# Seventh feature chunk of a token-mixing product as half-width products on TensorE column tiles

## The chip, the cores and the metric

The kernel runs on one core of one Trainium2 chip. The metric is device time in microseconds (us) of one execution. Most executions of one kernel agree within 0.3%. Every comparison of times below is made on one chip, against runs of the kernel before in the same series; traces of different series come from different chips. "Span" is the profiled stretch from the first to the last instruction of one execution; the device time is longer than it by 1.7 us or more, and I call that remainder the time outside the span. It is known to about 0.05 us only, because the spans of unprofiled executions are listed to 0.1 us.

## The reference

The program is a linear-attention block followed by a gated MLP that mixes tokens. Only the last part matters for the change (S = 2048 tokens, D = 512, F/2 = 896 features):

```python
def _B_ref(x, w_in, w_sp, b_sp, w_out):
    z  = _gelu(jnp.einsum('bsd,df->bsf', x, w_in))
    z1 = z[..., :Fh].copy()
    z2 = _layernorm(z[..., Fh:], axis=-1)
    g  = jnp.einsum('ts,bsf->btf', w_sp, z2) + b_sp[None, :, None]   # token mixing
    return jnp.einsum('bsf,fd->bsd', z1 * g, w_out)
...
h  = x + _A_ref(_layernorm(x), A_wqkv, A_wo)        # attention
h2 = h + _B_ref(_layernorm(h), B_w_in, B_w_sp, B_b_sp, B_w_out)
```

The token mixing is a product of 2048x2048 by 2048x896.

## The kernel before

The 896 features are seven chunks of 128. Six of them go in pairs through `cell`, which computes the 2x2 block product (two feature chunks, two token groups of 512) with seven half products instead of eight; the operands `t1, t2, t4` and `s1, s2, s4` are sums of blocks. The seventh chunk has no partner, and is multiplied plainly: sixteen matmuls for each of its token groups.

```python
    cnt = [0, 0]

    def gate(fc, tok, b, add):                     # VectorE: g = product + bias; z1 * g
        t, z = u_t[cnt[0] % 2], z1T[:, fc, tok]
        ...
    for p in range(NG // 2):                       # two halves of the work
        lo, hi = (slice(tg * GW, (tg + 1) * GW) for tg in (p, p + NG // 2))
        last = KF - 1
        for tok, b in ((lo, EB[0]), (hi, EB[1])):  # the seventh chunk, plain
            matmuls(bank(b), [(z2[:, s, last * P:KF * P], wsp[:, s, tok]) for s in range(NT)])
            gate(last, tok, b, bsp[:, tok])
        ...                                        # t1, t2, t4
        for k in range(HF):
            ...                                    # s1, s2, s4
            cell(k, lo, hi)                        # seven products on two chunks
```

Every engine runs its instructions in the order of one packed list of operation numbers, which is written into the kernel and was searched for by a tuner:

```python
ORDER = "c-jTQ17HvU00h8C..."   # (cut) order in which the operations are put on the engines
```

And TensorE is kept busy at the very start by 50 warm-up matmuls whose result nobody uses.

```python
    def warmup(n, ns, behind=None):
        def fn(pe):
            for _ in range(n):
                inst = pe.matmul(bank(7, P), lhsT=warm, rhs=warm, start=True, stop=True)
            return inst
        ...
    warmup(34, 103)          # and 16 more behind the first statistics
```

## Time and profile before

| | kernel before |
|---|---|
| device time, median of 3 | 230.52 us (229.92 to 230.79) |
| span of the profiled execution | 228.4 us |
| TensorE / VectorE / ScalarE busy | 97% / 76% / 48% |
| share of TensorE in the chain that ended last | 87% |
| token mixing, first and second half | 112 to 163 us, 163 to 205 us and beyond |

TensorE bounds the kernel; the prediction below shows the lines that say so. The cost that it takes for VectorE comes from this row of the groups (line, engine, operation, output and inputs, shapes, count, then busy us and mean ns of one, then idle time before it and what ended it):

```profile
L996 DVE TENSOR_TENSOR u<-psum,bsp 128x512 bf16<-128x512 f32 x16 | 11.0, 688 | 9.4 <-PE psum L402 9.2
```

An addition of 128x512 out of PSUM takes 688 ns. The records of some matmuls are missing from this trace (1168 of 1191), so counts of matmuls are not compared.

### The profile page before, as it was taken

The page shows a single profiled execution, that of the slowest core. Times are in us where ns is not written, and L with a number is a line of the kernel's source. Part 1 is how long each engine was busy: PE and PEld are TensorE (multiplying, and loading weights), DVE is VectorE, ACT ScalarE, POOL GpSimd, SP SyncE. Part 2 cuts the span into 40 slices and gives each one's busy share as a digit, 9 for nine tenths or more (in the row PEclk, how much of TensorE's full clock was granted, in tenths as well). Part 3 has the DMA queues.
Part 4 walks back from the last instruction along what each step waited for, and adds up shares of the span by engine and source line. Part 5 has one row for each costly group of instructions (what it writes and reads, how often), then busy time and mean ns, then how long its engine had stood idle before and what let it go on. Part 6 is the DMA issues. An engine that isn't in the chain of part 4 may idle for free.

```text
span 228.4 us, 3248 instructions
## 1 busy us (share of the span) xinstructions
PE 221.9 (97%) x1168; PEld 110.1 (48%) x1191; DVE 174.5 (76%) x349; ACT 108.5 (48%) x203; POOL 47.1 (21%) x134
## 2 busy tenths in 40 slices
PE   7999999999999999999999999999999999999995
PEld 7444444453344444544444444444455556555453
DVE  3899656638999786679998869864988985574395
ACT  5695753389989988999762010300021311122010
POOL 4444300000562694138820000000000000000000
PEclk9999999999999999999999999999999999999999
DMA  6736449927566244599904999200000002010004
GB/s 192 240 77 139 93 110 377 252 70 182 115 126 129 46 95 92 115 210 187 182 1 90 196 192 203 58 0 0 3 0 0 24 26 92 0 46 3 0 23 161
DMA packets 58896, 23.68 MB, mean 104 GB/s; under 512 B 48512, under 2 KB 58752, under 8 KB 58880
## 3 DMA queue, kind: packets, MB, share of 16 engines
q1 hardware_dynamic: 58176, 22.88, 44.2%
q10 hardware_dynamic: 704, 0.59, 0.9%
q8 instruction: 9, 0.15, 0.3%
q14 instruction: 7, 0.06, 0.1%
HBM read 7.47 MB, written 2.10 MB: 42 GB/s over the span
## 4 chain that ended last, share of the span: by engine, by line
PE 87%; DMA 4%; DVE 3%; ACT 3%; issue 1%; POOL 1%; SPq 1%; DVEq 0%
PE psum L402 69%; PE psum L659 6%; PE psum L813 6%; PE psum L816 4%; DMA x<-in_A_x_dram 2%; DMA hnT<-hn 1%; DVE st L510 1%; ACT ct L421 1%; SPq L432 1%; ACT pqT L421 0%; PE psum L724 0%; PE psum L680 0%; ACT z L421 0%; DVE h L988 0%; ACT sh L421 0%
## 5 line engine op out<-in xcount | busy, mean ns | idle before, releaser
L421 ACT ACTIVATE psum<-psum 128x256 f32<-128x256 f32 (+1 forms) x39 | 17.7, 468 | 86.7 <-PE psum L402 55.5
L402 PE MATMUL psum<-wsp,z 128*128 128x512 bf16 x201 | 47.8, 379 | 0.4
L402 PEld LDWEIGHTS psum<-wsp,z 128*128 128x128 bf16 x208 | 20.3, 98 | 23.0
L421 ACT ACTIVATE e<-psum 128x1024 bf16<-128x1024 f32 (+1 forms) x18 | 16.7, 927 | 14.1 <-PE psum L402 13.1
L402 PE MATMUL psum<-t,s 128*128 128x512 bf16 x95 | 22.3, 379 | 0.1
L402 PE MATMUL psum<-wsp 128*128 128x256 bf16 (+1 forms) x87 | 18.9, 313 | 0.2
L421 ACT ACTIVATE z1T<-psum 128x512 bf16<-128x512 f32 x28 | 15.7, 600 | 6.3 <-PE psum L402 5.7
L996 DVE TENSOR_TENSOR u<-psum,bsp 128x512 bf16<-128x512 f32 x16 | 11.0, 688 | 9.4 <-PE psum L402 9.2
L813 PE MATMUL psum<-win,hnT 128*128 128x512 bf16 x63 | 16.4, 379 | 0.3 <-DMA hnT<-hn 0.3
L402 PE MATMUL psum<-wout,z1T 128*128 128x256 bf16 (+1 forms) x81 | 16.2, 313 | 0.0
L659 PE MATMUL psum<-pk,xn 128*128 128x512 bf16 x64 | 15.3, 379 | 0.0
L402 PE MATMUL psum<-xnT,wqkv 128*128 128x512 bf16 x61 | 15.1, 379 | 0.2
L402 PE MATMUL psum<-m,pqT 128*128 128x512 bf16 x62 | 14.6, 380 | 0.4 <-DVE h L787 0.2
L402 PE MATMUL psum<-wqkv,xnT 128*128 128x512 bf16 x61 | 14.7, 379 | 0.2
L421 ACT ACTIVATE z<-psum 128x896 bf16<-128x896 f32 x16 | 14.4, 919 | 0.8 <-PE psum L816 0.5
L402 PEld LDWEIGHTS psum<-t,s 128*128 128x128 bf16 x96 | 9.4, 98 | 10.0
L581 DVE TENSOR_SCALAR e<-e 128x1024 bf16<-128x1024 bf16 (+1 forms) x18 | 7.0, 391 | 8.1 <-ACT e L421 7.9
L816 PE MATMUL psum<-win,hnT 128*128 128x384 bf16 x64 | 13.0, 326 | 0.0
L510 DVE BATCH_NORM_STATS2 st<-x 128x6 f32<-128x512 bf16 x15 | 9.9, 674 | 3.8 <-DMA x<-in_A_x_dram 3.8
L996 DVE TENSOR_TENSOR u<-psum,p 128x512 bf16<-128x512 f32 x12 | 8.3, 688 | 5.8 <-PE psum L402 5.8
L787 DVE SCALAR_TENSOR_TENSOR h<-psum,x 128x512 bf16<-128x512 f32 x16 | 10.7, 686 | 1.8 <-PE psum L402 1.7
L402 PEld LDWEIGHTS psum<-wsp 128*128 128x128 bf16 x90 | 8.7, 98 | 6.8 <-DVE wsp L1001 0.4
(126 smaller groups left out, 378.3 us busy)
## 6 DMA issues: line engine op xcount, KB each, us to landing
r<-rcp SPq DMA_DIRECT2D x16, 128.0 KB, 2.6
out_dram<-h SPq DMA_DIRECT2D x15, 128.0 KB, 1.7
win<-in_B_w_in_dram SPq DMA_DIRECT2D x2, 896.0 KB, 7.2
x<-in_A_x_dram SPq DMA_DIRECT2D x6, 256.0 KB, 4.3
wqkv<-in_A_wqkv_dram SPq DMA_DIRECT2D x2, 512.0 KB, 5.7
wout<-in_B_w_out_dram SPq DMA_DIRECT2D x1, 896.0 KB, 7.2
wo<-in_A_wo_dram SPq DMA_DIRECT2D x1, 512.0 KB, 5.9
bsp<-in_B_b_sp_dram SPq DMA_DIRECT2D x1, 512.0 KB, 4.4
```

The costliest lines, as they stand in the source:

```text
L402: inst = pe.matmul(out_ap, lhsT=a, rhs=b, start=start and i == 0, stop=stop and i == len(pairs) - 1, **kw)
L421: return g.add("ACT", lambda ac: ac.activation(out_ap, in_ap, func, **kw), [in_ap, *extra], [out_ap] + ([accum] if accum is not None else []),
L432: return g.add(eng, lambda q: q.dma_start(out_ap, in_ap), [in_ap], [out_ap], cost=issue, lat=lat, dma=name, **k)
L510: dve(lambda v: v.bn_stats(s[:, 0:6], src[:, n, :]), [src[:, n, :]], [s[:, 0:6]], D)
L581: dve(lambda v: v.tensor_scalar(e, e, 1.0, EPS_PHI, op0=ALU.min, op1=ALU.add), [e], [e], w * GW, acc=4)
L659: inst = pe.matmul(bank(CB[c]), lhsT=xn[:, i, c * P:(c + 1) * P], rhs=pk[:, i, :], start=i == 0, stop=i == NT - 1)
L787: dve(lambda v, n=n, b=b, s=s: v.scalar_tensor_tensor(h[:, n, :], bank(b), 1.0, x[:, n, :], op0=ALU.mult, op1=ALU.add, accum_out=s[:, 0:1] ...
L813: pe.matmul(bank(b), lhsT=hnT[:, c, n * P:(n + 1) * P], rhs=win2[:, c, 0:GW], start=c == 0, stop=c == KD - 1)
L816: inst = pe.matmul(bank(b + 1, F2), lhsT=hnT[:, c, n * P:(n + 1) * P], rhs=win2[:, c, GW:FH], start=c == 0, stop=c == KD - 1)
L996: dve(lambda v: v.tensor_tensor(t, bank(b), add, ALU.add), [bank(b), add], [t], GW, ps=True)
```

## The change

The seventh chunk is split into two pieces of 64 features, so that it too becomes a 2x2 block product with seven half products instead of eight. A product with 64 output features uses only half of the array's columns, so two of them are to run side by side, one on the lower and one on the upper column tile. The partial sums that land in the wrong half of the partitions are moved by ScalarE copies. The intent is 28 matmul slots for 32 in each half of the work.

```diff
+    s6 = [g.sbuf(f"s{j}c", ...) ...]            # s1, s2, s4 of 64 features
+    b2 = g.sbuf("b2", ...)
@@
-    load_x("SP", 0, 1, 2150)
+    load_x("SP", 0, 1, 2200)                    # (and other assumed load times)
@@
+    def halves(pairs, extra):
+        def fn(pe):
+            for s in range(max(len(a) for _, a, _ in pairs)):
+                for o, a, start in pairs:       # the two tiles take turns
+                    if s < len(a):
+                        inst = pe.matmul(o, lhsT=a[s][0], rhs=a[s][1], ...)
+            return inst
+        ...
+    def last_cell(lo, hi):
+        halves([(pb(Y, L), [(z2[:, s, fl], wsp[:, s, lo]) for s in ss], True),
+                (pb(X, U), [(s2[:, s, :], t2[:, s, :]) for s in ss], True)], 106)
+        halves([(pb(E, L), [(s1[:, s, :], t1[:, s, :]) for s in ss], True),
+                (pb(Y, U), [(z2[:, HT + s, fh], t4[:, s, :]) for s in ss], True)], 106)
+        act(b2[U], pb(Y, L), ACT.Copy, GW)      # across the partition halves
+        dve(... pb(X, U) = pb(X, U) + b2[U] ...)
+        act(pb(X, L), pb(X, U), ACT.Copy, GW)
+        for r in (L, U):
+            add(p5[c][r], E, L, hi)
+        halves([... four and four ...], 106)
+        halves([... eight and eight ...], 106)
+        add(b2[L], E, U, lo)
+        add(b2[U], X, U, lo)
+        gate(KF - 1, lo, Y, b2)
+        gate(KF - 1, hi, X, p5[c])
@@
-        last = KF - 1
-        for tok, b in ((lo, EB[0]), (hi, EB[1])):
-            matmuls(bank(b), [(z2[:, s, last * P:KF * P], wsp[:, s, tok]) for s in range(NT)])
-            gate(last, tok, b, bsp[:, tok])
@@
         for k in range(HF):
+            if k == C6[p]:                      # behind the other cells
+                ...
+                last_cell(lo, hi)
@@
-ORDER = "c-jTQ17HvU00h8C..."
+ORDER = "c-jrsLjoiQ00h9s..."                    # a new order of everything
```

More of the change, by code (lines that the diff above doesn't have):

```diff
@@ L15 @@
 SEM_NS = 45.0
-ORDER = "c-jTQ17HvU00h8Cwq47%ZQHhO+qGrewr$(CZ5wxy5Czc?4-pX=Q4t+65EHQw8*z{Txe$On$c?;6f}{Y5a0rjk2m>Q5gkT7T2ndM~2##b(juc3VL`aNO$cOwWi~>lD3aEsNXo|{cjQB{1)JTIOD2Q~(fTBo`Ldb-SD2C$5iYlmz%xHpU$bxFfhMLHZ66k@F=!tIVj#8+O9H@a>sDtKcftF~6Ug(X!=!4d%jkYL_x~PXSD1)-7k8x;#u~>%jIE;f>jw3jPHfV>q$cb_&kM`(*0T_sW=#P%*gw9xkrI>(;n1rL4jAJ-~6<CSYScT)5f`({>!5D;*2*fl@#dHk8X#`;?hG7lXVH8HA3%X(kW@0`TU=~hdA<kee*5eeO<0W2TvYuj!o?$lTU^qr#12$q27Go23U_0hw9yVhO_F@lqVjp&4H_qZ5wqhI3V?Pey3a;WBF5n`r;|4C_CNAR^UgHg3;Vo|CF7DwD?&AT1^Bo={1Vi!>BJe#v;WIwq2fpDa9^(l@F)YI{G`}M}BQg>{;tRgw7yck7!GDOw*bK+t_={9b&8UpVD2&WJ%*_0Z!RXAw0!%|QE6I3_!?=vkv`okJ%)pGy%hD9fupslXEVD5?b1)|hu`r9UD2uTc%dswlu{?7zfC-q8nK)Isxr8lQn{8N}^;nY0)rxJ|gFTsuiCKY3n3N^BhP_#b^|_c!xr}Ssnx&YG$yt$=SeaGWfK}O$jo6q?Sc558jVaWesnnDy)rTp$g{ifNTiK3j)Qf$&m%}-NHQ9pI*`6KPk^R`8oj8D<*^E;d$n=`ZAdciVPUCcD)fvuUHxA?=4rUi-P)6<JC}z`Wj^RvZR$66II%QW*<<MEq;yRAya*pF{&f#2c=MK)}3XbPW9$_wJQf}o@KAqzP?&nZW;sGAydd_E8cIPxr<a7<=LQduoF5*!xU^30nOwH14&Cy)V(|j$^LM_rA=2Za|QehQQeic&*U13ob)G-#<U6xd7RaPl&U|GH4RbFFxz2$kn<9puYP9En8p5!i`;zk}~6CGwbRnQZbQ598GB|YUIR@WE)<uiWeH-=YmMNkM`;6FB14PE4OzThS9=4C?n`G60(iI4c5t5{VvRZCPIZDun?)CWe=YQE$vUgr(o<SqVSWJOU_N!CyP;zveTJyla}wNOjdReiNmYqe8I#ZY{;S99HF2X$5g1t_K-GnQg2m`*dHUh_9UF_c29joPY#x~QXis++p2lX|F;daJK?s-b$Rs~W4H`fGsVD6SGIng;1J2Wp7=D2&1?v63j9;_1AGX}B(EutsR4hH94rHA+dfQI|AYV>DLdwN;z6M-wzoleA8!wM}PqMf<c`o3&jJwL|N*Mr*ZS8+1{-bx>z@PJ4A!hqOfp^hk&GTu*dNM|4@obye4NLMQc9*Y!+6nyA})p&NRv@4BPAdaYA>qno;=#ag1JTBhY%p_N*tmx5pEp5E%6KI*<6=)FGahd$`1zUZ@R_?N!woBryz{wSqsIhgHK{-^p5?hx+i1`g>^4(%`w=SHsW2#)B~uIW0C=I9RV@UG>^j^Y@O=~%AnIF9XVuIK7*;<%3I_)g%2PU5Cc>}F2mhHmZvCvsY+b7v=WCntAfr*{TtbX{k5CTDSLXLnZTbT+qfZg+Jaw{;8Wa4r{gA?J5K7j{t>aTm9Aceipe7k4+8aA}uyNtbd@w{sbnb9;Ai4_9zy_jP&qbAR`8Z};(JPjMwr_h8TP5YO~%&+-5d^dL|3aZmMJ&+#zN^Fpupd~fgqZ}bR{^d@iiR&ViQFY*#^^G@&fcJFYIhkBRyc$CL_xJNtC<2>GDe8LmF)O)?p%e>zcJ;^71$_IVgXMENNyuvU1(yx5c%YEMGe8Go&#IJqSE4|jMyvC3H#Fu>8Pkq(bebcvn#n*hpw|vLXe9w3Nzz_Y_@BH2$oYW~?z<C|XQC-Cqeb~qR#_Rmt_r2PW{L%jbNviim"
@@ new lines @@
+ORDER = "c-jrsLjoiQ00h9stZm!2ZQHhO+qP}nwr$(CmAs)26&?{08L<%#5fBMc5Eao79Wf9Su@D#WkOR4p6S)Bpp%DUt5kN?UL2v{?A|ya!Bt#MfMKB~qG9*U|<UwBKLqViQ9K=UTq(XkALjj~gArwId6h>O4M`jd7IaEMKR780+Mng0~BUD0VG(|JCKyze56=XqmWJNJ_Ll+cBS9C`SR7EyaLk-kIYt%$bltgW`K`Ye3IFv$Zj7MFJ!C2J85-h_~EJt>fL0PmzTl7Fr^g?gcM+5XhUkpG$^v6I<KznpRM;yc<9L5n0#|VVNL`=pcOu;lv#R{y%Y8=He9LFl0Kv+!2It;>K48cf@!f13tXUxD%%*O%@#W0-28l1)~EW~Wg!FsI4DV)JGyu@Tp(Nj#-G`+w^Y``Wg!eVU44$Q?oY{nMs#UAX$F6_oxoWnkx$5w2^ejLCRT*Wn9z(ribO<cw;yv1w0!7JRxb=<&x+`}E*#RCLkPzK{WJj5fsM^c65Cw#zXJjN6J#7BI=H~c_2enohK{}7G8@CW2`gk&fNX9z}T41Px#{zhp2MPx=~Bt~EgiYb|qxtN!k7?n|&o2eL^aTt@an3`#rmg$(D`DkWl9_D8jW@R>JX9kvJfMr;UIarqQ7?(8|pS78jOW2$Vn2_aInl)LAi&=mLS%`&MgvD8hMcIO_Se_MFk(F4POId}j*^P;rgo&7x)!3cMn4CSihIQGJ%h-nXSf35pkd4@bYgvq2xRt%wo7>oy?bx0j*pbQAl#Mx*BRGsBIh><7nq#<}V>yo7xq~~og1fkq$&^A}Sb|kqoqIT)DV0il*^Es%gK0H|8I@X@G?kf^M$?!@S=EW@lwBE=US~L6Gn7L)l}9r*OS3gco!OPSG?UqMmgjh$eK?+d*^jf>pR+lElQ@T~IG6Kyf%7?l7nx7Fb%X_!SA|qi#Z*N3Rai$^RCichC3Tmjbc_SJkn6aQgSnmyIFUm*h;ucW6;(o|b%ka0hV!(D^OZykv`~vwN#%5vZ+VU7^@J7llx6jYfBB46^@U&gjmLR{8+ecR`GD8Ck(c<K`&mr~c#tP~h^zUI|9F}2`JJbDgCF>jHwiTo^@Fz<Mqw31)m1~4)mW!lOX1W+;nh@|_>hnIm@oK}uNXlQ6;xGJM>Q2i&D27*)m&{9M=e!XQ58%-`HR67LLnttq10B96iv4oSMAhM@wA)ql|Y9XT`{zot<+le)Jg5tU0u{w9n?(?)Kk6HSv}NH^|e{Q8Bk>PQ9>osC&pAP^;JKG)@u&XXU0}yt=4U=*A@*@FZI_+4bd<S)KHDkC~eblozh^9)=rJlSdG_F9n%_Z&_+$vIGxc1oz^66)eeo+Zk^M9-O*X?(pqiTCau!}9n>D})p6a`KAqPI-PZ#>(L-I-QytPJ9o9P?(MP@4WnIuC-P094(^Xy54ZYA!-O?vL)^oko8(r5cz1C-a)en8wFTK@Ieb5*E)?zKuQZ3VRt<XxX(m#Du5C`=iHL(0wcEBMV+`$~iO&r$Y+|)fB!Qma!p$+$PC^vLOM{+Yqb~MLu6i0P8$9617cTC51JST8MCvpoXF`d}Woy<u+)7_oiDV)-&oW{M~%30jl>D<~`o!;4<+G(B9nViEpoy)nM$BmrLJ)O^a-O~Bp#)VwO1zga@UCeD=*hO8&W!=FgUCQlT&gEUn?OnkYUD+Mo$$i|})m+0>+{Im8+kM^7{awogT-DWG)Ad}}13k!tJ;X!3(yKkpt9;bQeB38}!oxk=cfH2<Ji@1Z+9Q3&=Y7`GJ<8`i*5iD^<2~9FJ;pOU!IM1Ivpmgfz0Mas$CEw9>%GAneaV}>$#Xr=4}9PAy~Y3j&vU!CdV#lju@`!omw2fcdAV2kvUhricl)Yu__`nZkso`P_n3hz-s@}L=jVRnr@rOe-fsmC`;edcr(gJ`U-`9v`L_@FkKg#6Klqd1`n^B;yTAF1KRb@=xV}p}v*SC1OZevh;75GWe|^V490&vn1PufWe0A`^e|U=oX8"
@@ L315, in bass_sequential_preLN__linear_attn_block__mixer_gmlp__prompt_kernel @@
     HT, HF = NT // 2, KF // 2
+    O_ST = 1024
     TB, SB = HT * GW * 2, HT * P * 2
@@ L337, in bass_sequential_preLN__linear_attn_block__mixer_gmlp__prompt_kernel @@
             for k, o in enumerate((o_win + KD * FH * 2, o_win, o_pk + TB))]
+    s6 = [g.sbuf(f"s{j}c", o, [HT, P // 2], BF16) for j, o in enumerate((o_win + KD * FH * 2 + 3 * SB, o_win + 3 * SB, o_c + O_ST))]
+    b2 = g.sbuf("b2", o_pk + TB + 3 * SB, [GW], FP32)
+    assert TB + 3 * SB + GW * 4 <= KD * S * 2 and 3 * SB + HT * P <= KD * FH * 2
     p5 = [g.sbuf(f"p5{b}", o_ct + 2 * TB + b * GW * 4, [GW], FP32) for b in range(2)]
@@ L373, in bass_sequential_preLN__linear_attn_block__mixer_gmlp__prompt_kernel @@
     warm = const("warm", [P], BF16)
+    cc[0] = o_c + O_ST
     st = [const(f"st{k}", [NT, 8], FP32) for k in range(2)]
@@ L487, in load_x @@
         return first_load(eng, x[:, n:n + w, :], x_d[n * P:(n + w) * P, :], f"x{n}", lat, behind)
-    load_x("SP", 0, 1, 2150)
-    load_x("ACT", 1, 1, 2300)
-    x2 = load_x("SP", 2, 1, 2300)
-    load_x("ACT", 3, 1, 2550)
-    first_load("SP", wqkv[:, 0:2, D:2 * D], A_wqkv[0:2 * P, D:2 * D], "wka", 4200)
-    wk = first_load("ACT", wqkv[:, 2:4, D:2 * D], A_wqkv[2 * P:4 * P, D:2 * D], "wkb", 4400)
-    for n, lat, behind in ((4, 4600, None), (6, 3400, x2), (8, 3850, wk), (10, 4000, wk), (12, 4200, wk), (14, 4400, wk)):
+    load_x("SP", 0, 1, 2200)
+    load_x("ACT", 1, 1, 2350)
+    x2 = load_x("SP", 2, 1, 2350)
+    load_x("ACT", 3, 1, 2600)
+    first_load("SP", wqkv[:, 0:2, D:2 * D], A_wqkv[0:2 * P, D:2 * D], "wka", 4800)
+    wk = first_load("ACT", wqkv[:, 2:4, D:2 * D], A_wqkv[2 * P:4 * P, D:2 * D], "wkb", 5000)
+    for n, lat, behind in ((4, 5200, None), (6, 4000, x2), (8, 2500, wk), (10, 2700, wk), (12, 3700, wk), (14, 3900, wk)):
         load_x("SP", n, 2, lat, behind)
@@ L989, in mo_pair @@
             store(n, slice(0, D), h[:, n, :])
-    cnt = [0, 0]
+    cnt, C6 = [0, 0], (2, 2)
     def gate(fc, tok, b, add):
@@ L1023, in cell @@
         gate(k + HF, lo, B, bsp[:, lo])
+    def halves(pairs, extra):
+        def fn(pe):
+            inst = None
+            for s in range(max(len(a) for _, a, _ in pairs)):
+                for o, a, start in pairs:
+                    if s < len(a):
+                        inst = pe.matmul(o, lhsT=a[s][0], rhs=a[s][1], start=start and s == 0, stop=s == len(a) - 1,
+                                         skip_group_check=True)
+            return inst
+        return PE(fn, [v for _, a, _ in pairs for ab in a for v in ab], [o for o, _, _ in pairs], len(pairs[0][1]) * 216 + extra)
@@ new lines, in last_cell, with add @@
+    def last_cell(lo, hi):
+        c = cnt[1] % 2
+        cnt[1] += 1
+        X, Y, E = 6, 7, EB[c]
+        H = P // 2
+        s1, s2, s4 = s6
+        f0 = (KF - 1) * P
+        fl, fh = slice(f0, f0 + H), slice(f0 + H, f0 + P)
+        L, U = slice(0, H), slice(H, P)
+        ss = range(HT)
+        pb = lambda b, r: psum[r, b, :]
+        q = range(HT // 2)
+        def add(o, b, r, i):
+            dve(lambda v: v.tensor_tensor(o, pb(b, r), bsp[r, i], ALU.add), [pb(b, r), bsp[r, i]], [o], GW, ps=True)
+        halves([(pb(Y, L), [(z2[:, s, fl], wsp[:, s, lo]) for s in ss], True),
[3 more added lines that the diff above has]
+        act(b2[U], pb(Y, L), ACT.Copy, GW)
+        dve(lambda v: v.tensor_tensor(pb(X, U), pb(X, U), b2[U], ALU.add), [pb(X, U), b2[U]], [pb(X, U)], GW, ps=True)
+        act(pb(X, L), pb(X, U), ACT.Copy, GW)
+        for r in (L, U):
+            add(p5[c][r], E, L, hi)
+        halves([(pb(Y, L), [(z2[:, HT + s, fl], wsp[:, HT + s, lo]) for s in q], False),
+                (pb(E, U), [(z2[:, HT + HT // 2 + s, fl], wsp[:, HT + HT // 2 + s, lo]) for s in q], True)], 106)
+        halves([(pb(X, L), [(s4[:, s, :], wsp[:, HT + s, hi]) for s in ss], False),
+                (pb(X, U), [(z2[:, s, fh], wsp[:, s, hi]) for s in ss], False)], 106)
+        add(b2[L], E, U, lo)
+        add(b2[U], X, U, lo)
+        gate(KF - 1, lo, Y, b2)
+        gate(KF - 1, hi, X, p5[c])
@@ L1038, in bass_sequential_preLN__linear_attn_block__mixer_gmlp__prompt_kernel @@
         for k in range(HF):
+            if k == C6[p]:
+                if p == 0:
+                    f0, H = (KF - 1) * P, P // 2
+                    x11, x21, x12, x22 = (z2[:, s:s + HT, f0 + j * H:f0 + (j + 1) * H] for s in (0, HT) for j in (0, 1))
+                    combine(s6[0], x21, x22, ALU.add)
+                    combine(s6[1], s6[0], x11, ALU.subtract)
+                    combine(s6[2], x12, s6[1], ALU.subtract)
+                    combine(x21, x11, x21, ALU.subtract)
+                last_cell(lo, hi)
             if p == 0:
```

## The prediction

> **What bounds the kernel now.** I read the page first: the busy shares and the chain of work that ended last.
>
> ```profile
> span 228.4 us, 3248 instructions
> PE 221.9 (97%) x1168; PEld 110.1 (48%) x1191; DVE 174.5 (76%) x349; ACT 108.5 (48%) x203; POOL 47.1 (21%) x134
> ...
> PE 87%; DMA 4%; DVE 3%; ACT 3%; issue 1%; POOL 1%; SPq 1%; DVEq 0%
> ...
> L402 PE MATMUL psum<-wsp,z 128*128 128x512 bf16 x201 | 47.8, 379 | 0.4
> L402 PE MATMUL psum<-t,s 128*128 128x512 bf16 x95 | 22.3, 379 | 0.1
> ```
>
> The chain is 87% TensorE. The two groups at the end are most of the token mixing (products of `wsp` with the gated half `z`, and the combined operands `t`, `s` of six feature chunks), and TensorE idled 0.4 and 0.1 us before them. The mean of 379 ns is the length of one pipelined record; what a matmul costs is the distance between starts. In the timeline sixteen stand between 123.78 and 127.23 us, so 3.45 / 16 = 0.216 us each.
>
> ```profile
> 123.78 3.62 PE L402 MATMUL psum<-wsp,z 128*128 128x512 bf16 x16
> 127.23 3.62 PE L402 MATMUL psum<-t,s 128*128 128x512 bf16 x15
> 130.69 3.62 PE L402 MATMUL psum<-wsp,z 128*128 128x512 bf16 x16
> 134.14 3.62 PE L402 MATMUL psum<-t,s 128*128 128x512 bf16 x16
> ```
>
> The first and third rows are the seventh chunk of the first half of the work (its two token groups of 512, sixteen matmuls each); TensorE goes from row to row without a hole. A table by stage shows how near the other engines are:
>
> ```profile
> core 0: us, PE busy (x) PEld busy (x) DVE busy (x) ACT busy (x) POOL busy (x), PEclk, DMA share, GB/s
> ...
> 112.00:163.00 51.00, 50.74 (x235) 23.08 (x239) 40.93 (x66) 10.23 (x20) 3.49 (x8) 1.00 0.48 90
> 163.00:205.00 42.00, 41.79 (x236) 23.32 (x239) 33.44 (x61) 7.61 (x19) 0.00 (x0) 1.00 0.08 26
> ```
>
> Token mixing of the first half lies in 112 to 163 us, the second half after it, mixed with output products. TensorE is full at clock 1.00, VectorE 80% busy (40.93 of 51, 33.44 of 42), ScalarE nearly free. So a TensorE slot saved here is time saved, as long as VectorE keeps up.
>
> The kernel already has matmuls on column tiles, the best evidence for this change: sixteen products of 32 columns, four to a tile row, between ordinary ones (timeline of TensorE):
>
> ```profile
> 43.52 1.03 PE L659 MATMUL psum<-pk,xn 128*128 128x512 bf16 x4
> 44.48 1.05 PE L680 MATMUL psum<-pk,ones 128*32 128x512 bf16 x16
> 45.46 1.04 PE L659 MATMUL psum<-pk,xn 128*128 128x512 bf16 x4
> ```
>
> From 44.48 to 45.46 us sixteen matmuls took 0.98 us: four slots of 0.216 (0.863) and 0.12 left over. So four tiles share one slot. The ordinary four before take 43.52 to 44.48, 0.96 instead of 0.863: 0.10 left over. Going into tile mode and back thus costs 0.10 + 0.12 = about 0.21 us per visit.
>
> **What the Trainium skill says.** (1) "TensorEngine Tiling (Array Packing)", Key Properties: tiles work independently, and changing the tiling mode drains the engine. The trace agrees on both, at 0.21 us for in and out. (2) "TensorE: Matmul & The Clock Gate", Measured speedup vs the span model: three column tiles gave 2.38 times, not 3. The trace is kinder in a stream (four tiles in one 0.216 slot), and it decides. (3) "PSUM — Partial Sum Buffer", PSUM bank collisions raise a hardware error: column tiles may write disjoint partitions of one bank at the same time. The change relies on this; the trace has it for four tiles of one bank. (4) "VectorE: DVE Perf Modes", Why PSUM operands drop a tier: fp32 from PSUM runs at the basic rate. The trace has 690 ns for 128x512 out of PSUM. Lanes are parallel, so I take the same 690 for an operation on 64 partitions (estimate; no half-partition row exists).
>
> **The change part by part.**
>
> *TensorE, removed.* Two token groups of 16 matmuls in each of two halves: 64 slots, 64 x 0.216 = 13.82 us.
>
> *TensorE, added.* The chunk is cut in two pieces of 64 features, and the same seven-product scheme as in the other cells runs on it. A 64-column product of eight contraction blocks takes half the array; two run side by side. Per half of the work four calls: 8, 8, 4 and 8 pairs (seven products, the seventh split into two sums of four). That is 28 slots for 32. If pairs share a slot, both halves take 56 x 0.216 = 12.10 us: 8 slots or 1.73 us saved.
>
> *TensorE, mode visits.* Two groups per half could mean four visits. I decoded the instruction order in the diff and numbered it against the old list. On TensorE the first two calls are adjacent in the first half, while the third and fourth are separated by ordinary cells; in the second half the first two are separated and the last two adjacent. That is three visits per half, six in all: 6 x 0.21 = 1.26 us. Net on TensorE: 1.73 - 1.26 = 0.47 us saved.
>
> *VectorE.* Per half five new operations of 512 fp32 from PSUM (one partial sum added, two halves of p5, two halves of the other bias sum): 5 x 0.69 = 3.45 us. The gates keep their number. In the first half four new combinations of 8x64 bf16; the trace has 420 ns for 512 bf16 elements, so 1.7 us. VectorE becomes about 40.9 + 5.2 = 46.1 of 51 us (90%), and 33.4 + 3.5 = 36.9 of 42 (88%).
>
> *ScalarE.* Two copies per half across partition halves, 584 ns each: 2.3 us on an engine 20% busy there.
>
> *The chain inside a new cell.* After the second call: copy 0.58, add 0.69, copy 0.58, and in the second half two p5 additions ahead on VectorE, 1.38: about 3.2 us. TensorE has ordinary work and the third call in that time (about 3.4 us in the second half, over 9 in the first, counted in slots from the decoded order). This just closes in the second half.
>
> *Lost filler.* The 32 plain matmuls needed no combined operand, so they bridged the four 2.28 us combinations of `t` (2.28 us per record). Now the first cells must come without them; I estimate 0.2 us of holes.
>
> *Reordering elsewhere.* The diff also alters assumed load latencies, and the whole order with them: another order of first statistics, the third weight load ahead of the first transposes, and input weights after more `wsp` loads. Before 16 us TensorE is busy 14.00 of 16, much of it warm-up, so a better order might win a few tenths; the later queue could cost as much. I put -0.2 there, with +-0.5.
>
> Sum: -1.73 + 1.26 + 0.2 - 0.2 = about -0.5 us. From 230.5: 230.0.
>
> **The rivals.**
>
> *Tiles do not overlap.* Then 112 half-width matmuls cost 112 x 0.216 = 24.2 us for 13.8 before, plus 1.26: +11.6 us, 242 us. Speaking for it: no 64-column row in the trace, and twice as many weight loads per slot. Against: the 32-column rows, with four loads and four matmuls in each slot. I give it 1%.
>
> *VectorE or the copy chain becomes the bound.* At 90% in the first half, with products that wait for operands only VectorE makes, TensorE could stand still 1 to 3 us: 231 to 233 us. For it: the lost filler and 5.2 us of added work in 51. Against: TensorE never waited 0.2 us for VectorE in this stage before, and the chunk has moved behind cells that keep TensorE fed. I give it 15% for over 1 us.
>
> *The saving is swallowed by mode visits.* If a 64-column visit costs 0.29 us rather than 0.21, the gain is nil: 230.4 us. This is quite possible and would not be told from the prediction by the time alone.
>
> *The reordered loads decide.* With a net effect of half a microsecond, a moved weight or transpose can outweigh the title of the change in either direction: 229 to 231.5.
>
> **Range and chances.** All likely outcomes lie within 1.5 us of the old time; runs before span 229.92 to 230.79. A gain of 2% would need 4.6 us, but the whole saving without any cost is 1.73. A loss of 2% needs the first rival, or a bad second or fourth. I take 230.0, range 228.9 to 231.4, and chances 0.01, 0.96, 0.03.
>
> **What would show it.** In the changed profile: matmul rows 128*64 whose pairs start together, with 0.216 us from pair to pair (step one); six visits with some 0.1 us lost on each side (step two); no TensorE idle before `t,s` rows above a few tenths (filler); VectorE near 46 us in the first token mixing stage; the start of that stage moved by under 0.5 us against before (reordering). The prediction is wrong if pairs come 0.43 us apart, if TensorE waits on the partition-crossing copies or on `t`, or if the start of the stage moves by more than a microsecond.

## More of the kernel before

All runs used here are in the fast state. The one run without a state is a single look, and says so.

## The result, and the profile after

The changed kernel took 230.56 us (median of 6 runs, 230.11 to 231.18), the kernel before in the same series 230.37 us (6 runs, 229.55 to 230.79). The ratio is 1.0017, with a 95% interval from 0.9993 to 1.0042: the same within 2%, and hardly to be told from no change at all. Ratios here are the mean time of one kernel's fast runs over that of the other's of the same rounds, so not quite the ratio of the medians that I quote.

The page of the changed kernel, with the busy line and the chain that ended last:

```profile
span 228.4 us, 3395 instructions
PE 223.0 (98%) x1239; PEld 109.5 (48%) x1239; DVE 183.9 (81%) x363; ACT 110.5 (48%) x207; POOL 48.8 (21%) x134
...
PE 89%; ACT 4%; DVE 2%; DMA 1%; POOL 1%; issue 1%
```

The span is the same to a tenth, TensorE is as full as before, and VectorE went from 76% to 81%. In the groups, the new products are those of L1036, 64 columns wide:

```profile
L407 PE MATMUL psum<-wsp,z 128*128 128x512 bf16 x144 | 34.0, 379 | 0.0
L407 PE MATMUL psum<-t,s 128*128 128x512 bf16 x96 | 22.0, 379 | 0.0
...
L1036 PE MATMUL psum<-wsp,z 128*64 128x512 bf16 x48 | 9.6, 382 | 0.0
...
L1055 DVE TENSOR_TENSOR b<-psum,bsp 64x512 f32<-64x512 f32 x4 | 2.8, 694 | 4.4 <-PE psum L1036 4.4
...
L426 ACT ACTIVATE b<-psum 64x512 f32<-64x512 f32 x2 | 1.2, 589 | 9.7 <-PE psum L1036 9.7
```

No TensorE idle stands before any of these matmul groups, the plain ones or the new ones. This column hides small losses, though: it counts from the modelled end of the matmul before (a record is 379 ns long, while starts are 216 ns apart), so a loss of under 0.16 us shows only in the distance of starts. A VectorE addition on 64 partitions takes as long as one on 128 (694 against 688 ns), as the prediction had assumed. How two tiles share a slot is seen in the timeline of TensorE (start, length, instruction):

```profile
133.63 1.03 PE L407 MATMUL psum<-wsp,z 128*128 128x512 bf16 x4
134.58 0.40 PE L1036 MATMUL psum<-wsp,z 128*64 128x512 bf16 x1
134.59 0.40 PE L1036 MATMUL psum<-t,s1c 128*64 128x512 bf16 x1
134.82 0.38 PE L1036 MATMUL psum<-wsp,z 128*64 128x512 bf16 x1
134.83 0.38 PE L1036 MATMUL psum<-t,s1c 128*64 128x512 bf16 x1
```

And at the end of the same visit:

```profile
137.85 0.38 PE L1036 MATMUL psum<-t,s0c 128*64 128x512 bf16 x1
137.85 0.38 PE L1036 MATMUL psum<-t,z 128*64 128x512 bf16 x1
138.16 1.04 PE L407 MATMUL psum<-t,z 128*128 128x512 bf16 x4
```

The two matmuls of a pair start 0.01 us apart, and later pairs follow each other every 0.216 us. At the entry, though, the first pair starts 0.309 us after the last ordinary matmul instead of 0.216 (0.09 lost), and at the exit the next ordinary matmul starts 0.312 us after the last one on the tiles (0.10 lost). The first pair's slot is 0.240 us long and the first ordinary one afterwards 0.226 (0.03 lost). Where the ordinary neighbours have 256 columns, they lose as much. Added up from the starts, a visit costs 0.226 us, and the six cost 1.36 us. The expectations further down have 0.24 a visit and 1.43 for six, a first count of mine that was a little too high. The stages (same stretches and columns as in the prediction):

```profile
112.00:163.00 51.00, 51.00 (x265) 22.75 (x265) 47.07 (x74) 11.91 (x23) 3.52 (x7) 1.00 0.42 84
163.00:205.00 42.00, 42.00 (x260) 23.01 (x259) 34.33 (x67) 8.91 (x22) 0.00 (x0) 1.00 0.08 26
```

VectorE (third busy number) went from 40.93 to 47.07 us in the first stretch, and TensorE stayed full. So the result is a saving that was spent again on TensorE itself. To see where, I measured the distance between landmarks that both traces have (from the starts of single matmul records, in us):

| from / to | before | changed | difference |
|---|---|---|---|
| start to first key-sum product (`pk,ones`) | 44.48 | 44.47 | -0.01 |
| to first `win,hnT` matmul (first input product of the MLP) | 19.68 | 19.91 | +0.23 |
| to last `win,hnT` matmul | 43.05 | 43.04 | -0.01 |
| to last matmul: token mixing and output, "the stage" below | 118.29 | 118.13 | -0.16 |
| to the end of the span | 2.86 | 2.83 | -0.03 |

The column tiles act only in the fourth line. There the ledger closes: 8 slots saved are -1.73, six visits are +1.36, one new hole is +0.14 (0.13 and a first slot that is 0.01 longer), and small stalls at 146, 162 and 212 us are +0.06. The sum is -0.17; the trace has -0.16. The hole is this one (timeline of VectorE, then of TensorE's weight loads; the bracket gives the idle time before and its releaser):

```profile
106.44 0.51 DVE L560 TENSOR_SCALAR z<-z,st,rs 128x896 bf16<-128x896 bf16 x1 [0.72 <-POOL rs L523]
...
106.99 0.67 DVE L867 TENSOR_TENSOR psum<-psum,p5z 128x512 f32<-128x512 f32 x1
...
107.71 0.11 PEld L407 LDWEIGHTS psum<-wsp 128*128 128x128 bf16 x2 [0.35 <-DVE psum L867]
```

In the new order VectorE stands still for 0.72 us for a GpSimd result, and the sum behind it reaches TensorE too late. The kernel before has no such hole.

### The profile page after: what moved, and what is told of

The parts are those of the page before. It is cut to its first block, busy times and chain, and to the rows that moved or that the text cites. A ratio compares the mean times of both kernels' runs of the same rounds, so it can differ in the third digit from the quotient of the medians.

```text
span 228.4 us, 3395 instructions
## 1 busy us (share of the span) xinstructions
PE 223.0 (98%) x1239; PEld 109.5 (48%) x1239; DVE 183.9 (81%) x363; ACT 110.5 (48%) x207; POOL 48.8 (21%) x134
## 4 chain that ended last, share of the span: by engine, by line
PE 89%; ACT 4%; DVE 2%; DMA 1%; POOL 1%; issue 1%
PE psum L407 65%; PE psum L664 6%; PE psum L818 6%; PE psum L1036 6%; PE psum L821 5%; ACT e L426 1%; DMA x<-in_A_x_dram 1%; DVE st L515 1%; DVE h L993 1%; ACT r L426 1%; POOL st L539 1%; ACT rcp L426 1%; PE psum L729 0%; PE psum L574 0%; ACT m L426 0%
## 5 line engine op out<-in xcount | busy, mean ns | idle before, releaser
L426 ACT ACTIVATE psum<-psum 128x256 f32<-128x256 f32 (+2 forms) x41 | 19.1, 472 | 75.2 <-PE psum L407 48.3
L407 PE MATMUL psum<-wsp,z 128*128 128x512 bf16 x144 | 34.0, 379 | 0.0
L407 PEld LDWEIGHTS psum<-wsp,z 128*128 128x128 bf16 x144 | 13.8, 98 | 15.8 <-issue 0.8
L407 PE MATMUL psum<-wsp 128*128 128x256 bf16 (+1 forms) x90 | 19.7, 315 | 0.0
L407 PE MATMUL psum<-wout,z1T 128*128 128x256 bf16 (+1 forms) x83 | 16.7, 315 | 0.0
L407 PE MATMUL psum<-m,pqT 128*128 128x512 bf16 x64 | 15.2, 380 | 0.8 <-DVE h L792 0.6
L407 PE MATMUL psum<-wqkv,xnT 128*128 128x512 bf16 x64 | 15.3, 379 | 0.4 <-ACT xnT L426 0.4
L539 POOL TENSOR_SCALAR st<-st 128x1 f32<-128x1 f32 x10 | 3.7, 370 | 46.1 <-ACT sh L426 32.5
L1001 DVE TENSOR_TENSOR u<-psum,p 128x512 bf16<-128x512 f32 x14 | 9.6, 689 | 4.6 <-PE psum L407 4.5
L1002 DVE TENSOR_TENSOR z1T<-u,z1T 128x512 bf16<-128x512 bf16 x28 | 11.6, 420 | 0.4
```

What stands on the lines that cost most here:

```text
L407: inst = pe.matmul(out_ap, lhsT=a, rhs=b, start=start and i == 0, stop=stop and i == len(pairs) - 1, **kw)
L426: return g.add("ACT", lambda ac: ac.activation(out_ap, in_ap, func, **kw), [in_ap, *extra], [out_ap] + ([accum] if accum is not None else []),
L539: pool(lambda p: p.tensor_scalar(s[:, 2:3], s[:, 0:1], s[:, 0:1], -1.0 / (n * n), op0=ALU.mult, op1=ALU.mult), [s[:, 0:1]], [s[:, 2:3]], 240)
L1001: dve(lambda v: v.tensor_tensor(t, bank(b), add, ALU.add), [bank(b), add], [t], GW, ps=True)
L1002: dve(lambda v: v.tensor_tensor(z, t, z, ALU.mult), [t, z], [z], GW, acc=2)
```

## The experiments

All twelve kernels gave correct results. The first series of four had the kernel before at a median of 230.31 us (11 runs), the second at 230.29, the third at 230.20 and the fourth at 230.22 (11 runs each). Theory one is the ledger above: sharing works, and each visit costs somewhat over 0.2 us. "Theory two" came later, and concerns instruction fetch.

### a_repeat: the changed kernel once more

No edit.

> The changed kernel once more, to see how far its landmarks repeat. In its first trace the last matmul of the hidden layer's second half starts at 107.42 us (before: 107.21) and the last matmul of all at 225.55 (before: 225.50). Theory one, the ledger: on TensorE the change saves 8 slots (1.73 us), pays six visits to tile mode at 0.24 us (1.43), so gains 0.30; the new instruction order upstream of token mixing loses 0.21 us before 107 us and 0.13 us in a hole right after it, so the end is unchanged. It expects the same landmarks within 0.1 us and 0.0 to 0.1% of the kernel before. Theory two, noise: the upstream landmarks wander by 0.2 us or more from run to run, and nothing was lost to the order; it expects landmarks elsewhere.

Measured: 230.60 us (230.11 to 231.39), ratio 1.0013 [0.9994, 1.0031]. The landmarks agree with the first trace to within 0.01 us, stage 118.13. One repeat makes the first stretch look steadier than it is: in e_eight, e_four2 and e_serial below, whose order is the same up to there and beyond, the first key-sum product came at 44.46, 44.69 and 44.82 us, and in e_oldhead and e_four, which share the old order, at 44.30 and 45.23. I have no cause for this, and it is as large as the effects in question. The second and third lines of the table are within 0.1 us of the changed kernel's in e_eight, e_four2 and e_serial. But the profiled run was 1.1 us longer at its tail: after the last matmul came 3.92 us instead of 2.83. In the timeline of SyncE one issue of an output store took 1.70 us:

```profile
224.68 1.70 SPq L437 DMA_DIRECT2D out_dram<-h  x1
```

The first trace has this issue at the same moment, with 0.43 us:

```profile
224.68 0.43 SPq L437 DMA_DIRECT2D out_dram<-h  x1
```

That was unexpected, and became theory two.

### e_oldhead and e_newhead: which part of the order costs

```diff
 # e_oldhead: the changed kernel, first 581 operations (all up to the MLP) in the order of before
-ORDER = "c-jrsLjoiQ00h9s..."
+ORDER = ...
 # e_newhead: the kernel before, those 581 operations in the changed order
-ORDER = "c-jTQ17HvU00h8C..."
+ORDER = ...
```

> The changed kernel with the first 581 operations of the schedule (up to about 107 us) put in the order of the kernel before; token mixing as changed. Theory one, the ledger: the upstream landmark returns to 107.2 us, the hole after it goes, and the last matmul starts at about 225.2 us, 0.3 us earlier than in the kernel before; time 0.1 to 0.2% below it. Theory two, VectorE: the gain is lost inside token mixing, where VectorE is 92% busy, and an earlier start there is eaten by waits: last matmul at 225.5, time equal to before, and holes of TensorE in front of products that need t or s.

> The kernel before (no tiles) with the first 581 operations in the order of the changed kernel. Theory one, the ledger: it pays the order alone, last matmul at about 225.85 us, 0.34 later than before, time 0.1 to 0.2% above it. Theory two, VectorE or noise: no change, last matmul at 225.5 within 0.1.

Measured: e_oldhead 230.70 us (230.31 to 231.30), ratio 1.0020 [1.0005, 1.0034]; e_newhead 230.62 us (230.16 to 230.75), ratio 1.0008 [0.9995, 1.0022]. From the first key-sum product to the first `win,hnT` matmul, e_newhead took 19.92 us like the changed kernel, while e_oldhead took not 19.68 but 20.15. So the old order does not simply restore the old time; it varies, with a wait of TensorE for a transpose (`hnT<-hn`) that lasted 0.44 us in the kernel before and 0.91 us in e_oldhead. At this point I gave up the reading that the new order loses 0.2 us ahead of the token mixing, as unproven; the padded kernels below bring it back with the cause. Theory one missed both ends: the last matmul came at 225.65 us in e_oldhead (expected 225.2) and at 226.12 in e_newhead (expected 225.85, but its first key-sum product was already 0.38 late), and the hole at 107 us stayed, with 0.10 us, in e_oldhead. What these two do show is the stage: 118.29 us in e_newhead, as before, and 118.15 in e_oldhead, within 0.03 of the changed kernel. The small gain in the stage belongs to the tiles and to the order within it.

### e_four: four visits, first attempt

```diff
 # the four half-tile calls of each half stand in two adjacent pairs: two visits instead of three
-ORDER = "c-jrsLjoiQ00h9s..."
+ORDER = ...      # first 581 operations as before, the rest searched with an estimate of all durations
```

> As the run with the old order upstream, but the order of token mixing and of the output stage searched again so that each half visits tile mode twice instead of three times (four visits in all, calls one and two adjacent, three and four adjacent), with no new operation and none removed. Theory one, the ledger, at 0.24 us a visit: 0.48 us less than with six, last matmul at about 224.7 us, time 0.3% below the kernel before. Rival: the ordinary products between the third and fourth call were hiding VectorE's chain (it is over 90% busy), so holes of TensorE take the place of the two visits, and the last matmul stays at about 225.2.

Measured: 231.92 us (230.91 to 232.87), ratio 1.0067 [1.0042, 1.0092]. Holes came, most of them not where the rival put them. Waits of weight loads between 112 and 122 us:

```profile
PEld psum L407 <- DVE z L560: 0.8, 1, 0.8
PEld psum L407 <- DVE psum L867: 0.7, 1, 0.7
PEld psum L407 <- ACT z1T L426: 0.6, 1, 0.6
```

The stage took 119.39 us, 1.24 longer than in e_oldhead, although two visits had gone. The search had moved work around the first token-mixing products, and there VectorE and ScalarE results came late: by the starts TensorE lost 0.47, 0.35 and 0.32 us at these three places. Two more holes, of 0.22 us at 147 and 0.24 at 157 us, lie near the third and fourth calls (149 us), where the rival had put them all. The kernel is a failed build of the right experiment: it shows that an order with fewer visits can lose far more than a visit is worth.

### e_eight and e_four2: visits counted up and down

```diff
 # e_eight: one whole product put between the two adjacent calls, in each half: eight visits
-ORDER = "c-jrsLjoiQ00h9s..."
+ORDER = ...
 # e_four2: four visits, searched only from the first token-mixing products on, with results for
 # TensorE wanted 0.3 us early; one VectorE sum near 107 us put ahead of a normalisation
-ORDER = "c-jrsLjoiQ00h9s..."
+ORDER = ...
```

> The changed kernel with eight visits to the column tiles instead of six (one more in each half: the two adjacent pairs of products parted by one whole product each), the order elsewhere nearly as it was. Theory one (each visit costs TensorE 0.24 us and nothing else is at stake): the stage from the last win,hnT matmul to the last matmul grows from 118.13 by 2 x 0.24 = 0.48 to 118.6, and the time by 0.5 to 231.1. Rival (the gaps at the visits are hidden elsewhere or only shift waits): the stage stays within 0.1 of 118.13.

> The changed kernel with four visits to the column tiles instead of six (the two pairs of each half adjacent in both halves), the order changed only from the first token-mixing products on, chosen so that VectorE's results come at least 0.3 us before TensorE needs them where possible, and the VectorE sum that held TensorE for 0.13 us at 107.7 us put ahead of a normalisation. Theory one: the stage from the last win,hnT matmul to the last matmul goes from 118.13 to 118.13 - 2 x 0.24 - 0.13 = 117.5, no TensorE waits of over 0.1 us in it, and the time to 230.60 - 0.6 = 230.0. Rival (grouping the visits only trades them for waits on VectorE, as in the first kernel with four visits): holes of 0.2 us and more take their place, the stage stays at 118.1 or above.

Measured: e_eight 231.04 us (230.85 to 231.51, 4 runs), ratio 1.0039 [1.0015, 1.0064]; stage 118.58. e_four2 230.12 us (229.89 to 231.16), ratio 1.0001 [0.9980, 1.0023]; stage 117.62. So the stage is

| visits | stage, us |
|---|---|
| 4 (e_four2) | 117.62 |
| 6 (changed; repeat) | 118.13; 118.13 |
| 8 (e_eight) | 118.58 |

The steps are 0.51 and 0.45 for two visits, or 0.24 for one on average. The gaps at entry and exit are 0.226 in each of these traces; the rest is small stalls that the order brings along. With 56 slots for 64, 0.226 a visit, and the hole and stalls read from each trace (0.15, 0.20 and 0.20 us), the stages come out at 117.62, 118.12 and 118.57. Theory one holds. A detail of my expectation fell: the 0.13 us hole at 107 us stayed in e_four2. I had moved the wrong one of two sums, the later one; the one that TensorE waits for still stood behind the normalisation. Without that 0.13 the expectation was 117.65.

### e_serial: are the tiles independent, or must the instructions alternate?

```diff
-            for s in range(max(len(a) for _, a, _ in pairs)):
-                for o, a, start in pairs:
+            for o, a, start in pairs:                       # one tile's matmuls, then the other's
+                for s in range(max(len(a) for _, a, _ in pairs)):
                     if s < len(a):
```

> The changed kernel with the two loops in the half-tile products swapped: all matmuls of one column tile, then all of the other, where the changed kernel takes them in turns. Theory one (two matmuls share a slot because they stand next to each other in the queue on different tiles): the 112 narrow matmuls take 0.216 us each, 56 slots more, 12.1 us, the span near 240.5. Rival (the tiles have queues of their own that fill up either way): the span stays within 1 us of 228.4.

Measured: 235.24 us in a single look (state unknown), span 233.2; the stage took 122.63 us, 4.50 more than in the changed kernel. That is neither 12.1 nor 0. The timeline of TensorE shows what lies between:

```profile
135.16 1.02 PE L1036 MATMUL psum<-wsp,z 128*64 128x512 bf16 x4
135.82 0.40 PE L1036 MATMUL psum<-t,s1c 128*64 128x512 bf16 x1
136.03 0.38 PE L1036 MATMUL psum<-wsp,z 128*64 128x512 bf16 x1
136.06 0.38 PE L1036 MATMUL psum<-t,s1c 128*64 128x512 bf16 x1
```

In the program all eight `wsp,z` matmuls of this call come before the first `t,s1c`. In the trace the first `t,s1c` (second tile) starts at 135.82, together with the fifth `wsp,z` and ahead of the sixth at 136.03. In the calls with only four matmuls for each tile, the two tiles started 0.014 us apart from the first matmul on. This looks as if up to four matmuls of one tile can be held back while those of the other start. By that reading, of a visit with eight matmuls each, four at its beginning and four at its end run alone, four slots too many; of the six visits five contain such calls: 5 x 4 x 0.216 = 4.3 us against 4.50 measured. The reading fits, but only this run bears on it. What is shown is that alternating is needed for full sharing, and that order within the queue alone does not decide when a matmul starts.

### e_pad and e_trim: the instruction stream of TensorE

Theory two. The traces list packets of kind "instruction", 16384 bytes each, on one queue. They come once per about 251 instructions of TensorE (215 to 290 in the six traces that I had by then; the expectation below gives the range of the kernel before alone). I take them for TensorE's instruction fetch. The kernel before ends after nine of them. With 48 more matmuls and their loads, the changed kernel has a tenth due in the last microseconds. In a_repeat it was recorded at 224.6 us, right at the slow store issue of 224.68; in e_four at 227.0, again beside an issue of 1.53 us; in e_oldhead at 229.7, after the last instruction of the span. In the first trace of the changed kernel, and later in e_four2, e_eight and e_serial, no tenth was recorded; yet the profiled runs of the last two were 2.07 and 2.04 us longer than their spans, so either the records end too early or something else adds to that time. The time outside the span was 1.68 to 1.81 us in all 44 runs of the kernel before in my four series, and more than 1.85 us in 22 of 35 runs of the kernels with tiles and unchanged warm-up (up to 2.79).

The warm-up gives a lever on the number of instructions without touching the work:

```diff
 # e_pad: the kernel before, more and smaller warm-up matmuls (100 instead of 50)
-                inst = pe.matmul(bank(7, P), lhsT=warm, rhs=warm, ...)
+                inst = pe.matmul(psum[0:64, 7, 0:64], lhsT=warm[:, 0:64], rhs=warm[:, 0:64], ...)
-    warmup(34, 103)          # second: 16
+    warmup(68, 51)           # second: 32
 # e_trim: the changed kernel, fewer and wider ones (13 instead of 50), on another buffer of 512
-                inst = pe.matmul(bank(7, P), lhsT=warm, rhs=warm, ...)
+                inst = pe.matmul(bank(7), lhsT=warm[:, 0:P], rhs=warm, ...)
-    warmup(34, 103)          # second: 16
+    warmup(9, 412)           # second: 4
```

> The kernel before, with its 50 warm-up matmuls at the start made 100 smaller ones (64x64 instead of 128x128), so that TensorE has 2483 instructions in the records instead of 2383, while the rest is untouched. Theory two (instruction fetch): in the traces so far a 16384-byte packet of kind instruction comes once per 231 to 286 TensorE instructions (mean 251); the kernel before ends after nine of them, and the runs with 2481 to 2507 instructions had a tenth at 224.6, 227.0 and 229.7 us in three of four traces. It expects a tenth packet here too, between 222 and 231 us, the time outside the profile's span up from 1.69-1.78 us to 2.0 or more in half of the runs or more, and so 230.5 to 230.7 against 230.3, with the stage from the last win,hnT matmul to the last matmul still 118.29. Rival (the lost time outside the span comes from the tile visits themselves): no change, time outside the span 1.7, time within 0.1 of before.

> The changed kernel with its 50 warm-up matmuls (128x128) made 13 wider ones (128x512), so that TensorE has 2433 instructions in the records instead of 2507; all else as changed. Theory two expects no tenth instruction packet, time outside the span 1.7 us in every run instead of 1.7 to 2.8, no output-store issue of 1.5 us or more, and so a time 0.3 us below the changed kernel's 230.60: 230.3, the same as before within 0.1. The stage stays 118.13. Rival: the extra fetch has no effect on the time, 230.6, and the time outside the span stays spread from 1.7 to 2.8.

Measured for e_pad: 230.31 us (229.95 to 231.75), ratio 1.0011 [0.9985, 1.0036]; the time outside the span was 1.70 to 1.97 us, above 1.85 in two of six runs, and no tenth packet was recorded. The packets moved as the theory says (the first to 7.4 us from 13.3), but the expected loss of 0.3 us did not come: a miss for the size. Measured for e_trim: 231.17 us (230.84 to 232.14), ratio 1.0045 [1.0025, 1.0066], slower instead of 0.3 us faster. The time outside the span behaved as expected, 1.68 to 1.77 us in all six runs, and no tenth packet came. What spoiled it is ahead of the token mixing, where TensorE now waited 0.77 us at 70.8 us by the distance of starts (the bracket below, which counts from the modelled end, has 0.61). The timeline of SyncE in e_trim has the transpose, that of TensorE the wait:

```profile
68.81 1.82 SPq L440 DMA_TRANSPOSE hnT<-hn  x1
```

```profile
71.56 0.81 PE L818 MATMUL psum<-win,hnT 128*128 128x512 bf16 x3 [0.61 <-DMA hnT<-hn]
```

The same issue in the changed kernel:

```profile
68.87 1.27 SPq L440 DMA_TRANSPOSE hnT<-hn  x1
```

Having fewer warm-up instructions moved a packet from 61.3 us to 68.5 us, onto this transpose. Its issue took 0.55 us longer, and TensorE, which waits for that transpose, paid for it. This coincidence is regular: in the twelve traces other than the last two below, all issues of `hnT<-hn` transposes that took more than 1.40 us (1.46 to 2.75, where 1.19 to 1.36 is usual) lie beside such a packet, among them the one of the kernel before at 60.94 us (1.81 us, packet at 61.1). Not every packet beside a transpose costs something; several beside issues of 1.2 us did not.

### e_all: four visits and the short warm-up together

```diff
 # e_four2's order and e_trim's warm-up
```

> The same four visits and order, and the 50 warm-up matmuls made 13 wider ones, so that TensorE has 74 instructions fewer. Theory one and two together: the stage 117.5, no tenth instruction packet, time outside the span 1.7 us, and so 230.60 - 0.6 - 0.3 = 229.7, which would be 0.6 us (0.26%) below the kernel before. Rival: the parts do not add up, 230.0 or above.

Measured: 230.90 us (230.37 to 231.27), ratio 1.0028 [1.0007, 1.0049]. The rival was right: the stage was 117.62 as wanted and the time outside the span at most 1.80 us in all six runs, but the packet fell on the same transpose (issue 2.04 us), and TensorE stood still for 1.20 us at 71 us. The profile names a ScalarE sum as the last releaser there, so that it was the transpose is read across from e_trim.

### e_pad4 and e_pad4old: four visits, and the packets moved away

```diff
 # e_pad4: e_four2's order and e_pad's warm-up (100 small matmuls)
 # e_pad4old: the same, first 581 operations in the order of before
```

> The changed kernel with four visits and the new order (as the last four-visit kernel, stage 117.62), and its 50 warm-up matmuls made 100 smaller ones, so that TensorE has some 100 instructions more. In the traces the SyncE transposes of hn take 1190 to 1300 ns, and those of 1460 to 2750 ns all coincide with a 16384-byte instruction packet of TensorE's queue; the padding moved those packets 6 to 12 us earlier in the kernel before. Theory (the packets' places decide the stages ahead of 107 us and the last stores): packets near 51, 76, 102, 128, 153, 175 and 196 us and the tenth near 216 us, none from 222 us on; no output store issue over 1.0 us; time outside the span at most 1.80 us in all runs; stage 117.6; last matmul near 224.9 to 225.2, span 227.8 to 228.1, time 229.5 to 229.8 against 230.2, so 0.2 to 0.3% below the kernel before. Rival (the head wanders for other reasons): time outside the span up to 2.5 us as in the four-visit kernel and the time 230.1.

> As the padded four-visit kernel, but with the first 581 operations in the order of the kernel before (in the padded kernel before, the first win,hnT matmul came 19.35 us after the first z product, against 19.68 unpadded and 19.9 to 20.0 in the changed orders). Theory: last win,hnT matmul at 107.24 as in the padded kernel before, stage 117.65, last matmul 224.9, span 227.75, time 229.45 to 229.6, about 0.3% below the kernel before. Rival: stage 117.65 but the stages ahead at 107.5 to 107.9 again, time 229.9 to 230.1.

Measured: e_pad4 230.50 us (230.30 to 230.95), ratio 1.0018 [0.9999, 1.0037]. e_pad4old 229.43 us (229.09 to 229.97) against 230.22, ratio 0.9968 [0.9950, 0.9985]. The first missed its 229.5 to 229.8, although stage, packets and time outside the span (1.78 us at most) were as expected. The second is 0.8 us or 0.3% faster than the kernel before. Its page and its stages:

```profile
span 227.7 us, 3474 instructions
...
q8 instruction: 10, 0.16, 0.4%
```

```profile
112.00:163.00 51.00, 50.50 (x262) 22.97 (x265) 47.44 (x74) 11.79 (x23) 3.49 (x7) 1.00 0.47 91
163.00:205.00 42.00, 41.79 (x259) 22.82 (x261) 33.72 (x63) 8.21 (x19) 0.00 (x0) 1.00 0.07 23
```

The ten packets are all there, the last at 215.5 us instead of in the final stores, and the time outside the span was 1.69 to 1.78 us in all twelve runs of the pair. The stage took 117.75 us in e_pad4old (0.13 more than in e_four2, because of a hole of 0.13 us at 114.0) and 117.62 in e_pad4.

The two differ ahead of 107 us, and this tells the two orders of the head apart. From the first key-sum product to the first `win,hnT` matmul, nine traces with the new order took 19.90 to 20.00 us, wherever the packets fell. The old order took 19.36 us in e_pad4old and 19.35 in e_pad, where no packet lies on the transpose at 61 us; and 19.68, 19.85 and 20.15 in the kernel before, e_four and e_oldhead, where the records have one beside the transposes there (in e_oldhead no transpose issue there was over 1.30 us, so how that one cost 0.8 us is open). So the old order is the better one by 0.55 us in this piece, and the kernel before enjoys only part of that. In e_pad4, in addition, the first key-sum product came at 45.12 us instead of 44.63 in e_pad4old; these 0.49 us are the unexplained wander of the first stretch, not the order.

Against the kernel before, the trace of e_pad4old has +0.15 us up to the first key-sum product, -0.32 to the first `win,hnT` matmul, 0.00 to the last, -0.54 in the stage and +0.07 in the tail: -0.64 in the span. Padding alone (e_pad) and four visits alone (e_four2) gained nothing measurable in time; only with both and the old head is the sum seen. In the trace of e_pad, 0.33 us won ahead of the first `win,hnT` matmul were lost again in the first stretch (44.84 us), which wanders.

## Why the prediction was right

The prediction was 230.0 us, the same within 2%; the result was 230.56, in the range. Its steps one by one:

- *Slots.* Right. Pairs start together and 0.216 us apart, no TensorE idle stands before them, and 8 slots or 1.73 us are saved. e_serial shows that this rests on the alternation of the two tiles: without it, the stage lost 4.50 us.
- *Six visits at 0.21.* The number was right, the size slightly low: 0.226 each, 1.36 us in place of 1.26. Four, six and eight visits give 117.62, 118.13 and 118.58 us. The 32-column tiles of the kernel before, which the estimate came from, were a good guide. The net on TensorE is thus -0.37 instead of -0.47.
- *VectorE.* Right on the whole: from 112 us to the end of the span it grew by 96.74 - 88.30 = 8.4 us, where the prediction's two terms add up to 8.7. They lie otherwise than expected, more in the first stretch (47.07, expected 46.1) and less in the second (34.33, expected 36.9), where part of the work slipped behind 205 us. Half-partition operations took 681 to 709 ns, estimated 690.
- *The chain with copies across partitions.* It did not hold TensorE. The rival of VectorE as the bound did not come in the changed kernel; e_four shows that it was near, since another order lost over a microsecond to late results of VectorE and ScalarE.
- *Lost filler, 0.2.* It cost nothing: idle before the `t,s` row is 0.0. The first ordinary cells that had to bridge the sums did so.
- *Reordering, -0.2 with +-0.5.* The sign was wrong. The order ahead of the MLP cost +0.23 us in the profiled runs (and 0.55 against the old order when that is undisturbed), and the hole at 107.7 us with the small stalls another 0.20. Both lie within the stated uncertainty.
- *Not in the prediction at all.* The longer instruction stream. Mean time outside the span was 1.90 us in the changed kernel's six runs, against about 1.75 before: some 0.15 us. Trimming (12 runs) and padding so that the last packet came early (12 runs) brought it to 1.80 or less in every run. The padded kernels with four visits have the longest streams of all, so what matters seems to be where the last packet falls, and not the length as such; how a late packet lengthens the end is inferred from three traces, and e_pad, which should have shown it in the kernel before, showed it only weakly.

So the sum of -0.5 us became about 0: -0.37 for tiles with visits, +0.20 and +0.23 for the order, and some +0.15 after the span, which makes +0.2, the measured difference of the medians (230.56 - 230.37 = 0.19). That agreement should not be pressed, for the interval of the ratio alone is 1.1 us wide. Nor does the number 230.0 prove much: its range, 228.9 to 231.4, also holds a kernel that gains nothing. What the runs confirm are the steps on TensorE; that the total stayed near the old time is partly luck, as the wander of the first stretch is as large as the net effect. The rival "the saving is swallowed by mode visits" was four fifths true: 1.36 of 1.73 us (its "nil: 230.4" should read 230.5).

## What to carry to other kernels

Half-width products on column tiles pay by the slot, but each change of tile mode has a price of its own (here a little more than one matmul of 512 columns), so count the visits in the final instruction order, not the calls in the source, and let both tiles take turns. When two parts of a change cancel to a few tenths of a microsecond, the order around them decides: check each new wait of the full engine, and mistrust a comparison whose head wanders by more than the effect. Adding instructions also moves where the instruction stream is loaded; if a time moves without any wait to explain it, look where those packets fall beside DMA issues that something waits for.

## What the Trainium skill lacked or had wrong

- "TensorEngine Tiling (Array Packing)", Key Properties, says that changing the tiling mode drains the engine, without a cost. Here one visit, in and out, costs 0.226 us by the starts of the matmuls (stages of 117.62, 118.13 and 118.58 us for four, six and eight visits).
- "TensorE: Matmul & The Clock Gate", The mechanism, says that matmuls start in strict program order. In e_serial a matmul of the second column tile started at 135.82 us, ahead of one on the first tile that comes before it in the program and started at 136.03.
- The same page, Measured speedup vs the span model, has 2.38 times for three column tiles. In a stream two tiles of 64 columns took one slot of 0.216 us per pair, twice the rate, with the loss only at entry and exit. No section says that the two tiles must alternate in the queue for this; not doing so cost 4.50 us.
- "Runtime: NRT & Kernel Launch", Instruction fetch mechanics, has the refills in blocks of 16 KiB, or 256 instructions, and calls their cost mostly hidden; the traces agree on the size (16384 bytes per some 250 TensorE instructions, every 17 to 29 us). It does not say that other DMA work beside a refill can take longer: issues of transposes beside such a packet took up to 2.75 us here instead of 1.19 to 1.36.
